# Shared row loads, ten token tiles and one weight sequence in a convolution, MoE and gated-FFN kernel

## The chip, the cores and the metric

The kernel runs on one core of one Trainium2 chip. The metric is the device time of one execution in microseconds. Engines are named as in the profile: PE (TensorE matmul), DVE (VectorE), ACT (ScalarE), POOL (GpSimd), SP (SyncE, which issues all DMAs here).

## The reference

Three layers run one after the other on x of shape (2, 4160, 192). `weight_gen` has shape (2, 4160, 8, 7); d_ff is 1024. The weights of the two feed-forward layers are float64 in memory.

```python
# 1: a causal convolution whose 7 taps differ by token and head
w = softmax(weight_gen, axis=-1)
out = np.einsum('bshk,bskhg->bshg', w, windows_of_7(x))
# 2: token mix, squared ReLU, gate
xk = mu_k * x + (1.0 - mu_k) * x_prev;  xr = mu_r * x + (1.0 - mu_r) * x_prev
k = np.maximum(xk @ w_k, 0.0)
x = sigmoid(xr @ w_r) * (k * k @ w_v)
# 3: a 3-tap convolution along the tokens as the gate of a hidden layer
h = np.maximum(x @ w_in, 0.0)
out = (h * sigmoid(conv3(h, conv_w))) @ w_out
```

## The kernel before

The 4160 tokens of each of the two batches are cut into nine tiles, one of 256 and eight of 488 (lines 15 to 25). Everything is planned by the function of line 169 in units of an abstract time: `at(t, fn)` files an operation under a priority `t`, a tile takes 16 units (line 733), a batch 8, a slice of 128 of the 1024 hidden columns 1. `Program.schedule` (line 101) then orders all operations with a cost for each (line 74): an engine that becomes free takes the operation with the lowest `t` of those that are ready, whether or not a lower one is still to come. What it puts out is a fixed order for each engine's queue.

The work of a tile:

- *Softmax* of the tap weights (line 370): group 0 is tile 0, group 1 is tile 1, group 2 all of tiles 2 to 8 in single instructions. Groups 0 and 1 have scratch of their own, group 2's lies in `stage` (line 232), the space of the weights on their way in.
- *Attention* (lines 402 to 430): `win_load` gives each partition, for two tokens 128 rows apart, all 7 rows of each window (2 x 1344 elements); `att_mul` multiplies two tokens at once, four adds sum the taps into `tok`. Two window buffers. Tile 0's first batch is on DVE, the rest on POOL (lines 717, 720, 736).
- *Mixing* (line 436): PE transposes the tokens into a bank `pa`, ACT shifts them by one token into `att`, DVE forms the two mixes in `mk`, ACT rounds them to the high part, POOL subtracts for the low part; what is left over of the 192 columns goes by DMA into `xB`.
- *First layer* `moe1` (line 526): per slice 5 matmuls into one of two banks `pa`, three ACT steps (ReLU, square, round), one DVE subtraction, 5 matmuls into `am`, `ar`. `gate_r` and `mix_out` put the result into `x2`.
- *Second layer* `moe2` (line 621): per slice 5 matmuls into one of two banks `pc`, ReLU on ACT, the three taps (one on ACT, two on DVE), sigmoid on ACT, product on DVE, rounding on ACT, subtraction on DVE, 5 matmuls into `bm`, `br`. It follows the first layer ten units later (`LAG`).
- *Carry* (line 573) copies the last two columns of `x2` to its front, on POOL.

So one slice through both layers costs 20 matmuls, 7 ACT and 5 DVE instructions. All products are split into a high and a low part.

Each weight is fetched in chunks of 512 or 384 columns into one of two raw buffers of `stage` (line 206), `narrow` (line 271) turns float64 into float32 by one ACT and five DVE instructions in the banks `bm`, `br` and `pc`, and `split` (line 285) writes the high part with ACT and the low part with DVE. Sixteen chunks: `w_k` 3, `w_v` 4, `w_r` 1, `w_in` 3, `conv_w` 1, `w_out` 4, at the priorities of lines 718 to 730. SP issues the loads of windows and weights, the DMAs of `xB` and the stores in one queue.

Of the kernel before, what the change touches and what calls it, by code (L numbers as in the profile page):

```python
# [15 lines left out]
FIRST = 256  # L16
NTILE = 9
REST = (SEQ - FIRST) // (NTILE - 1)
SIZES = [FIRST] + [REST] * (NTILE - 1)
# [4 lines left out]
SLOTS = [2] + [4] * (NTILE - 1)  # L24
# [11 lines left out]
class Program:  # L36
# [7 lines left out]
    def engine(self, name):  # L44
        program = self

        class Engine:
            def __getattr__(self, method):
                return lambda *a, **k: program.ops.append((name, method, a, k, program.now))

        return Engine()
# [22 lines left out]
    def cost(self, eng, method, out, ins, pointer):  # L74
# [21 lines left out]
        if eng == "POOL":  # L96
            busy = 0.06 + (n / 490 if method == "tensor_tensor" else n / 270)
            return busy, busy + 0.16
        return 0.6, 0.6

    def schedule(self):
        n = len(self.ops)
        succ, left, ready, dur, late, moved = [[] for _ in range(n)], [0] * n, [0.0] * n, [0.0] * n, [0.0] * n, [0.0] * n
        log = {}
        for i, (eng, method, a, k, _) in enumerate(self.ops):
# [4 lines left out]
            if method == "dma_start":  # L110
                moved[i] = self.count(out) * out.ap[0][1] * 4 / 200e3 if self.space(out) != "DRAM" else self.count(ins[0]) * ins[0].ap[0][1] * 4 / 200e3
# [18 lines left out]
        free = dict.fromkeys(self.real, 0.0)  # L130
        wires = dict.fromkeys(self.real, 0.0)
# [20 lines left out]
        for i in sorted(range(n), key=lambda i: (start[i], i)):  # L152
            eng, method, a, k, _ = self.ops[i]
            getattr(self.real[eng], method)(*a, **k)  # L154
# [14 lines left out]
def conv_moe_kernel(ctx: ExitStack, tc: tile.TileContext, xp, wg_first, wg_rest, mus, w_k, w_v, w_r, w_in, conv_w, w_out, out):  # L169
# [35 lines left out]
    stage = new("stage", [128, 4608], U32)  # L205
    raw_r = Ring([stage[:, 1024 * j:1024 * j + 1024].rearrange("p (a b) -> p a b", b=2) for j in (0, 1)])
    wy_r = Ring([stage[:, 2048 + 512 * j:2560 + 512 * j] for j in (0, 1)])
    wx_r = Ring([stage[:, 3072:3584]])
    wb_r = Ring([stage[:, 3584:4608].rearrange("p (a b) -> p a b", a=2).bitcast(F32R)])
    win_r = ring("win", 2, [128, 2, WIN])  # L210
# [15 lines left out]
    soft_at = [0, slots[0], slots[0] + slots[1], sum(slots)]  # L226
# [3 lines left out]
    for j in range(3):  # L230
        n = soft_at[j + 1] - soft_at[j]
        flat = new(f"smz{j}", [128, 2 * n * NH]) if j < 2 else f(stage)[:, :2 * n * NH]
# [11 lines left out]
    def at(t, fn):  # L244
        plan.append((t, len(plan), fn))
# [9 lines left out]
    def fetch(w, parts, n):  # L255
# [8 lines left out]
        else:  # L264
            st["x"] = f(wx_r())
# [26 lines left out]
    def prep_in(t, src, A, B, twin):  # L292
        st = {}

        def rem():
            st[0] = fetch(src, lambda w, k: [(64 * h, 64 * h + 64, 0, cols(w, k, 128, 192, 512 * h, 512)) for h in range(2)], 512)

        def rem2():
            x = narrow(st[0], 512)
# [12 lines left out]
        def main(c):  # L312
            st[1 + c] = fetch(src, lambda w, k: [(0, 128, 0, cols(w, k, 0, 128, 512 * c, 512))], 512)

        def main2(c):
            sl = slice(512 * c, 512 * c + 512)
            split(A[:, 0, sl], A[:, 1, sl], narrow(st[1 + c], 512))

        at(t[0], rem)
        at(t[1], rem2)  # L320
        for c in range(2):
            at((t[1] - 1.95, t[1] + 0.02)[c], lambda c=c: main(c))
            at(t[2 + c], lambda c=c: main2(c))

    def prep_out(t, src, W):
        st = {}
        for c in range(4):
            def load(c=c):
                st[c] = fetch(src, lambda w, k: [(0, 128, 0, w[256 * c:256 * c + 256, :].rearrange("(k p) d -> p k d", p=128))], 2 * DM)

            def go(c=c):
                x = narrow(st[c], 2 * DM).rearrange("p (k d) -> p k d", k=2)
                k = slice(2 * c, 2 * c + 2)
                split(W[:, k, 0, :], W[:, k, 1, :], x[:, :, 0:128])
                split(W[:, k, 2, 0:64], W[:, k, 2, 64:128], x[:, :, 128:192])

            at(t[c] - 1, load)
            at(t[c], go)

    def prep_r(t):  # L340
        st = {}

        def load():
            st[0] = fetch(w_r, lambda w, k: [(0, 128, 0, cols(w, k, 0, 128, 0, DM))]
                          + [(64 * h, 64 * h + 64, k * DM, cols(w, k, 128, 192, 0, DM)) for h in range(2)], 2 * DM)

        def go():
            x = narrow(st[0], 2 * DM)
# [4 lines left out]
        at(t - 1, load)  # L353
        at(t, go)

    def load_conv(t):
        st = {}

        def load():
            st[0] = fetch(conv_w, lambda w, k: [(0, 128, 0, w)], 3 * NF)  # L360

        def go():
            DVE.tensor_copy(cw.rearrange("p k n -> p (k n)"), narrow(st[0], 3 * NF))

        at(t, load)
        at(t + 1, go)

    def softmax(j, wg, eng, load, times):  # L370
        w, m, z = sm[j]
        P, n = PART[min(j, 1)], w.shape[1]
        w, m, z = w[:P], m[:P], z[:P]

        def s0():
# [442 lines left out]
```

## Time and profile before

| | |
|---|---|
| time, median of 3 runs | 827.6 us (825.28 to 828.04) |
| the profiled execution | 829.09 us, of which the span of the trace is 827.3 us |
| busy in the span | PE 703.2, PE weight loads 579.4, DVE 633.2, ACT 637.3, POOL 461.7 us |
| mean granted TensorE clock | 0.950 |
| DMA | 73.09 MB, of which the window loads are 34 of 1344 KB |

Read the time by stretch first: shares over the whole span mix a ramp in which weights are prepared, a long steady part and a tail. A matmul's busy time contains its pipeline, so the pace is read from the number of matmuls in a stretch, not from the time of one. Nearly every instruction has line 154, where the planner puts it out, so groups are told apart by tile names. In a timeline the bracket says how long the engine stood idle before the instruction and what ended that.

### The profile page before, as it was taken

The page shows a single profiled execution, that of the slowest core. Times are in us where ns is not written, and L with a number is a line of the kernel's source. Part 1 is how long each engine was busy: PE and PEld are TensorE (multiplying, and loading weights), DVE is VectorE, ACT ScalarE, POOL GpSimd, SP SyncE. Part 2 cuts the span into 40 slices and gives each one's busy share as a digit, 9 for nine tenths or more (in the row PEclk, how much of TensorE's full clock was granted, in tenths as well). Part 3 has the DMA queues.
Part 4 walks back from the last instruction along what each step waited for, and adds up shares of the span by engine and source line. Part 5 has one row for each costly group of instructions (what it writes and reads, how often), then busy time and mean ns, then how long its engine had stood idle before and what let it go on. Part 6 is the DMA issues. An engine that isn't in the chain of part 4 may idle for free.

```text
span 827.3 us, 9620 instructions
## 1 busy us (share of the span) xinstructions
PE 703.2 (85%) x3162; PEld 579.4 (70%) x3162; DVE 633.2 (77%) x1018; ACT 637.3 (77%) x1264; POOL 461.7 (56%) x250
## 2 busy tenths in 40 slices
PE   0145654689899999999999999999999999999775
PEld 0044543578668888888888888788888888888553
DVE  7765858876886878788778878787888787877754
ACT  1244645597797989898989889898989898989653
POOL 3499314586899697898987888969311010100000
PEclk9996787798999999999999999999999999999967
DMA  7654740012423423326126123430020002000000
GB/s 278 215 162 136 231 107 0 1 52 102 151 55 129 152 62 139 134 66 202 59 94 201 75 77 134 134 133 19 19 50 19 1 20 48 19 1 19 0 19 19
DMA packets 24370, 73.09 MB, mean 88 GB/s; under 512 B 3072, under 2 KB 13696, under 8 KB 24192
## 3 DMA queue, kind: packets, MB, share of 16 engines
q1 hardware_dynamic: 24320, 72.47, 26.8%
q8 instruction: 25, 0.41, 0.2%
q14 instruction: 25, 0.20, 0.1%
HBM read 55.45 MB, written 6.39 MB: 75 GB/s over the span
## 4 chain that ended last, share of the span: by engine, by line
PE 61%; DVE 18%; ACT 14%; POOL 4%; issue 2%; DMA 1%; SPq 1%; ACTq 0%; DVEq 0%; POOLq 0%
PE pa L154 18%; PE pc L154 15%; PE am L154 9%; PE bm L154 7%; PE ar L154 6%; DVE pc L154 5%; PE br L154 5%; POOL win L154 3%; ACT h L154 2%; DVE stage L154 2%; ACT g L154 2%; ACT pa L154 2%; ACT x L154 2%; ACT pc L154 1%; DVE g L154 1%
## 5 line engine op out<-in xcount | busy, mean ns | idle before, releaser
L154 DVE SCALAR_TENSOR_TENSOR pc<-h,cw,pc 128x488 f32<-128x488 f32 (+2 forms) x288 | 201.5, 700 | 41.5 <-ACT pc L154 38.4
L154 POOL TENSOR_TENSOR win<-win,sw 128x2688 f32<-128x2688 f32 x33 | 197.7, 5991 | 28.7 <-DMA win<-in_x_dram 28.6
L154 ACT ACTIVATE pa<-pa 128x488 f32<-128x488 f32 (+1 forms) x288 | 155.2, 542 | 53.1 <-PE pa L154 49.8
L154 PE MATMUL bm<-g,wo 128*128 128x488 f32 (+2 forms) x432 | 145.6, 386 | 26.7 <-ACT g L154 26.7
L154 PE MATMUL am<-s,wv 128*128 128x488 f32 (+1 forms) x432 | 144.8, 392 | 25.0 <-ACT s L154 23.0
L154 POOL TENSOR_TENSOR win<-win 128x384 f32<-128x384 f32 (+1 forms) x99 | 153.9, 1575 | 1.5
L154 DVE TENSOR_TENSOR pc<-h,pc 128x488 f32<-128x488 f32 (+2 forms) x144 | 92.3, 641 | 57.6 <-ACT pc L154 56.7
L154 PE MATMUL pa<-xA,wkA 128*128 128x488 f32 (+1 forms) x432 | 120.9, 388 | 15.7 <-DVE mk L154 9.2
L154 PE MATMUL pc<-x,wiA 128*128 128x490 f32 (+2 forms) x432 | 121.2, 385 | 2.4 <-DVE g L154 2.4
L154 PEld LDWEIGHTS bm<-g,wo 128*128 128x128 f32 x432 | 82.5, 195 | 48.2 <-ACT g L154 35.1
L154 DVE TENSOR_TENSOR s<-pa,s 128x488 fp32r<-128x488 f32 (+1 forms) x144 | 91.1, 634 | 30.0 <-ACT s L154 27.6
L154 PEld LDWEIGHTS am<-s,wv 128*128 128x128 f32 x432 | 83.1, 199 | 43.4 <-ACT s L154 28.9
L154 PE MATMUL ar<-s,wv 128*128 128x488 f32 (+1 forms) x288 | 109.4, 389 | 4.1 <-ACT x L154 2.9
L154 PE MATMUL br<-g,wo 128*128 128x488 f32 (+2 forms) x288 | 109.5, 381 | 1.4 <-DVE ob L154 1.4
L154 DVE TENSOR_TENSOR g<-pc,g 128x488 fp32r<-128x488 f32 (+2 forms) x144 | 91.5, 636 | 21.7 <-ACT g L154 20.8
L154 ACT ACTIVATE h<-pc 128x490 f32<-128x490 f32 (+2 forms) x144 | 81.3, 565 | 31.5 <-PE pc L154 26.3
L154 PEld LDWEIGHTS pa<-xA,wkA 128*128 128x128 f32 x432 | 80.9, 198 | 31.3 <-ACT xA L154 8.0
L154 ACT ACTIVATE pc<-h,cw 128x488 f32<-128x488 f32 (+2 forms) x144 | 94.4, 656 | 1.5
L154 PEld LDWEIGHTS pc<-x,wiA 128*128 128x128 f32 x432 | 80.6, 195 | 17.3 <-DVE g L154 4.7
L154 ACT ACTIVATE pc<-pc 128x488 f32<-128x488 f32 (+2 forms) x144 | 78.2, 543 | 15.2 <-DVE pc L154 15.1
L154 POOL TENSOR_TENSOR xA<-mk,xA 128x488 fp32r<-128x488 f32 (+1 forms) x36 | 42.3, 1185 | 84.5 <-ACT xA L154 84.5
L154 PE MATMUL pa<-xB,wkB 128*128 128x488 f32 (+1 forms) x288 | 86.7, 381 | 1.9 <-DMA xB<-mk 1.8
(89 smaller groups left out, 1005.9 us busy)
## 6 DMA issues: line engine op xcount, KB each, us to landing
win<-in_x_dram SPq DMA_DIRECT2D x34, 1344.0 KB, 6.0
xB<-rm SPq DMA_DIRECT2D x32, 122.0 KB, 2.3
xB<-mk SPq DMA_DIRECT2D x32, 122.0 KB, 2.3
out_dram<-om SPq DMA_DIRECT2D x14, 244.0 KB, 2.1
out_dram<-ob SPq DMA_DIRECT2D x14, 122.0 KB, 2.3
sw<-in_rest_dram SPq DMA_DIRECT2D x1, 1568.0 KB, 13.5
stage<-in_moe_w_v_dram SPq DMA_DIRECT2D x4, 384.0 KB, 3.5
stage<-in_moe_w_out_dram SPq DMA_DIRECT2D x4, 384.0 KB, 3.1
```

The costliest lines, as they stand in the source:

```text
L154: getattr(self.real[eng], method)(*a, **k)
```

## The change

- Ten tiles: 256, 248, seven of 472, 352. The two short tiles have two token slots a partition, the last has three.
- Neighbouring tokens lie on one partition: for L tokens it loads L + 6 rows once (`rows`), and each token multiplies its 7 rows into one buffer `prod`; three adds sum the taps. Transposes write with a step of L columns. All attention is on POOL.
- Softmax in four groups: tile 0, tile 1, tile 2, and tiles 3 to 9. The last is loaded late and worked in pieces of one tile each; its scratch lies in `stage`.
- All weight chunks form one sequence with three raw buffers; a chunk's load comes right behind the use of the chunk three before it. `wb` lies in `x2[1]`.
- Mixing of tiles 0 and 1 scales the shifted tokens on ACT and needs one DVE step fewer; for tile 0 the mixes lie in the banks `am` and `ar` and DVE forms the low parts. The carry is on ACT.
- The planner knows a start time for an operation (`hold`), ACT's table loads, and that POOL and a DVE instruction with two SBUF inputs exclude each other; its costs for POOL and DMA are changed.

The diff, cut:

```diff
-SIZES = [FIRST] + [REST] * (NTILE - 1)
+SIZES = [256, 248] + [472] * 7 + [352]
-SLOTS = [2] + [4] * (NTILE - 1)
+SLOTS = [2, 2] + [4] * 7 + [3]
...
-            busy = 0.06 + (n / 490 if method == "tensor_tensor" else n / 270)
-            return busy, busy + 0.16
+            busy = 0.1 + (n / 455 if method == "tensor_tensor" else n / 270)
+            return busy, busy + 0.12
...
+            shares[i] = eng == "POOL" or eng == "DVE" and (
+                src == ["SBUF", "SBUF"] or method in ("tensor_scalar", "tensor_copy") and self.space(out) == "SBUF" and src == ["SBUF"])
...
+            if shares[i]:
+                t = max(t, port)
+                port = t + dur[i]
+            turn = 0.0
+            if eng == "ACT" and self.ops[i][1] == "activation" and self.ops[i][2][2] in (ACTF.Exp, ACTF.Sigmoid):
+                turn = 0.0 if self.ops[i][2][2] == table else 1.3
+                table = self.ops[i][2][2]
...
-    raw_r = Ring([stage[:, 1024 * j:1024 * j + 1024].rearrange("p (a b) -> p a b", b=2) for j in (0, 1)])
+    raw_r = Ring([stage[:, 1024 * j:1024 * j + 1024].rearrange("p (a b) -> p a b", b=2) for j in range(3)])
-    win_r = ring("win", 2, [128, 2, WIN])
+    rows_r = ring("rows", 2, [128, max(SLOTS) + PAD, DM])
+    prod = new("prod", [128, WIN])
...
-    soft_at = [0, slots[0], slots[0] + slots[1], sum(slots)]
+    soft_at = [sum(slots[:j]) for j in (0, 1, 2, 3, NTILE)]
...
+    def prepare(first, seq):
+        for j, (t, (load, n, go)) in enumerate(seq):
...
+            at(first[j] if j < 3 else seq[j - 3][0] + 0.001, ld)
+            at(t, use)
...
+    def attention(i, b, t_load, t, dt_, eng, hold=(0.0, 0.0)):
+        L = SLOTS[i]
+        def load():
+            rows_t[i, b] = rows_r()[:, :L + PAD]
+            row = b * (SEQ + PAD) + STARTS[i] - EXTRA[i]
+            SP.dma_start(out=rows_t[i, b], in_=bass.AP(tensor=xp.tensor, offset=xp.offset + row * DM, ap=[[L * DM, PART[i]], [1, (L + PAD) * DM]]))
+        def token(l):
...
+            eng.tensor_tensor(p.rearrange("p (k g h) -> p k g h", k=KS, h=NH),
+                              rows_t[i, b][:, l:l + KS].rearrange("p k (g h) -> p k g h", h=NH), w, op=ALU.mult)
+            eng.tensor_tensor(y[:, 0:3], y[:, 0:3], y[:, 3:6], op=ALU.add)
+            eng.tensor_tensor(y[:, 0:2], y[:, 0:2], y[:, 2:7:4], op=ALU.add)
+            eng.tensor_tensor(tok_t[i][:, l, b * DM:b * DM + DM], y[:, 0], y[:, 1], op=ALU.add)
...
-                PE.transpose(p[:, l * P:(l + 1) * P], x[:P, l, k:k + 128], ident[:P, :P])
+                PE.transpose(p[:, l:l + SLOTS[i] * (P - 1) + 1:SLOTS[i]], x[:, l, k:k + 128], ident)
...
+            st[k] = (am_r, ar_r)[k]() if i == 0 else mk_r()
+            if i < 2:
+                a = shifted(lambda y, x: ACT.activation(y, x, ACTF.Copy, scale=onemu[:, own]))
+                DVE.scalar_tensor_tensor(out=st[k][:, :N], in0=st["p"], scalar=mu[:, own], in1=a, op0=ALU.mult, op1=ALU.add)
...
-            POOL.tensor_tensor(y, st[k][:, :N], f(x[:, 0, :N]), op=ALU.subtract)
+            (POOL if i else DVE).tensor_tensor(y, st[k][:, :N], f(x[:, 0, :N]), op=ALU.subtract)
...
-                POOL.tensor_copy(x2[b][:, :, 0:2], f(x2[b][:, :, n:n + 2]))
+                ACT.copy(x2[b][:, :, 0:2], f(x2[b][:, :, n:n + 2]))
...
+    attention(0, 0, -99.9, -90, 0.1, POOL)
+    attention(0, 1, -99.6, -83.7, 0.1, POOL)
+    prepare((-99.75, -99.7, -99.4), [(-82, chunk_rem(w_k, wkB, True)), (-81, chunk_in(w_k, wkA, 0)),
+                                     (-0.5, chunk_out(w_v, wv, 0)), (0.4, chunk_out(w_v, wv, 1)), (1.0, chunk_in(w_k, wkA, 1)),
+                                     (1.4, chunk_out(w_v, wv, 2)), (2.4, chunk_out(w_v, wv, 3)), (3.4, chunk_r()),
+                                     (4.4, chunk_rem(w_in, wiB, False)), (5.0, chunk_in(w_in, wiA, 0)), (6.0, chunk_out(w_out, wo, 0)),
+                                     (6.4, chunk_conv()), (7.0, chunk_in(w_in, wiA, 1)), (8.0, chunk_out(w_out, wo, 1)),
+                                     (9.0, chunk_out(w_out, wo, 2)), (10.0, chunk_out(w_out, wo, 3))])
+    softmax_load(3, wg_rest[:, (slots[1] + slots[2]) * KH:], 10.2, 40.0)
+    for j in range(NTILE - 3):
+        a, b = (sum(slots[3:3 + k]) for k in (j, j + 1))
+        softmax(3, a, b, POOL, (16.5 + 0.3 * j, 16.6 + 0.3 * j, 19.5 + 0.1 * j, 20.5 + 0.5 * j, 20.6 + 0.5 * j, 24.9 + 16 * j), None)
...
-                attention(i, b, T - 19.3 + 4.5 * b, T - 15 + 4.5 * b, 2.25, POOL)
-            for u, t in ((0, T - 5), (2, T - 3.7), (1, T + 3)):
+                attention(i, b, T - 22 + 4.5 * b, T - 15 + 4.5 * b, 1.125, POOL, (25.0 + 8 * b if i == 1 else 0.0, 0.0))
+            for u, t in ((0, T - 5), (2, T - 3.7), (1, T + 3)) if i > 1 else ((0, 7), (2, 8.3), (1, 15)):
                 mixing(i, u, t, 2.5)
```

## Rows read from the trace of the kernel before

**Rows 1.** Busy time by stretch: from:to, length, busy (instructions), clock, DMA, GB/s.

```profile
0.00:160.00 160.00, 67.70 (x302) 55.64 (x303) 114.83 (x191) 68.75 (x162) 82.93 (x50) 0.84 0.47 146
160.00:240.00 80.00, 72.39 (x359) 59.51 (x358) 61.00 (x114) 64.85 (x141) 66.54 (x31) 0.96 0.26 87
240.00:760.00 520.00, 515.50 (x2341) 430.18 (x2340) 416.96 (x654) 467.71 (x897) 312.20 (x171) 1.00 0.24 81
760.00:827.00 67.00, 47.56 (x166) 34.06 (x164) 40.42 (x62) 36.03 (x67) 0.00 (x0) 0.82 0.04 12
```

**Rows 2.** Timeline of PE, neighbouring matmuls of 256 columns: start us, us, operation, tiles, shapes.

```profile
164.51 0.28 PE L154 MATMUL bm<-g,wo 128*128 128x256 f32 x1
164.63 0.28 PE L154 MATMUL br<-g,wo 128*128 128x256 f32 x1
```

**Rows 3.** Waits of SP's queue: us in total, times, longest us.

```profile
SPq L154 <- POOL tok L154: 195.3, 26, 21.4
```

**Rows 4.** Timeline of SP: start us, us, engine, line, operation.

```profile
69.48 14.29 SPq L154 DMA_DIRECT2D stage<-in_moe_w_in_dram  x4
```

**Rows 5.** Timeline of DVE: start us, us, operation, tiles, shapes, count, [idle before].

```profile
5.83 0.39 DVE L154 TENSOR_TENSOR sw<-sw,smz 128x224 f32<-128x224 f32 x1
8.15 2.96 DVE L154 TENSOR_TENSOR win<-win,sw 128x2688 f32<-128x2688 f32 x1 [1.93 <-DMA win<-in_x_dram]
...
14.08 5.67 DVE L154 TENSOR_TENSOR win<-win 128x384 f32<-128x384 f32 x1
...
77.23 0.57 DVE L154 TENSOR_SCALAR br<-br 128x384 uint32<-128x384 uint32 x1 [2.75 <-ACT br L154]
...
126.45 5.76 DVE L154 TENSOR_REDUCE stage<-sw 128x448 f32<-128x3136 f32 x1
...
140.03 0.28 DVE L154 TENSOR_TENSOR wo<-br,wo 128x128 fp32r<-128x128 f32 x1
```

**Rows 6.** Timeline of POOL.

```profile
13.49 5.84 POOL L154 TENSOR_TENSOR win<-win,sw 128x2688 f32<-128x2688 f32 x1 [12.07 <-DMA win<-in_x_dram]
...
132.30 6.84 POOL L154 TENSOR_TENSOR sw<-sw,stage 128x3136 f32<-128x3136 f32 x1 [26.76 <-DVE stage L154]
...
153.70 6.92 POOL L154 TENSOR_TENSOR sw<-sw,stage 128x3136 f32<-128x3136 f32 x1 [12.17 <-DVE stage L154]
160.71 12.00 POOL L154 TENSOR_TENSOR win<-win,sw 128x2688 f32<-128x2688 f32 x2
```

**Rows 7.** Groups by shape, attention on POOL.

```profile
L154 POOL TENSOR_TENSOR win<-win,sw 128x2688 f32<-128x2688 f32 x33 | 197.7, 5991 | 28.7 <-DMA win<-in_x_dram 28.6
...
L154 POOL TENSOR_TENSOR win<-win 128x384 f32<-128x384 f32 x66 | 66.5, 1022 | 0.5
```

**Rows 8.** Groups by shape, weight chunks on DVE: busy us, mean ns | idle before.

```profile
L154 DVE SCALAR_TENSOR_TENSOR stage<-stage,pc 128x384 f32<-128x384 uint32 x9 | 5.0, 550 | 0.2
L154 DVE SCALAR_TENSOR_TENSOR stage<-stage,pc 128x512 f32<-128x512 uint32 x6 | 4.1, 682 | 0.1
```

**Rows 9.** Groups by shape, ACT and DVE on the two tile sizes.

```profile
L154 ACT ACTIVATE pa<-pa 128x488 f32<-128x488 f32 x256 | 143.6, 564 | 35.6 <-PE pa L154 32.6
...
L154 DVE SCALAR_TENSOR_TENSOR pc<-h,cw,pc 128x256 f32<-128x256 f32 x32 | 15.6, 486 | 5.0 <-ACT pc L154 4.5
...
L154 ACT ACTIVATE pa<-pa 128x256 f32<-128x256 f32 x32 | 11.6, 371 | 17.5 <-PE pa L154 17.2
...
L154 DVE TENSOR_TENSOR s<-pa,s 128x256 fp32r<-128x256 f32 x16 | 6.6, 420 | 10.9 <-ACT s L154 10.8
```

**Rows 10.** Timeline of PE in the tail, two slices apart.

```profile
804.40 0.71 PE L154 MATMUL bm<-g,wo 128*128 128x490 f32 x2 [2.01 <-ACT g L154]
...
812.17 0.71 PE L154 MATMUL bm<-g,wo 128*128 128x490 f32 x2 [2.01 <-ACT g L154]
```

**Rows 11.** Timeline of ACT around the big exponential.

```profile
139.77 1.28 ACT L154 ACT_TABLE_LOAD   x1
141.06 2.82 ACT L154 ACTIVATE sw<-sw 128x3136 f32<-128x3136 f32 x1
143.90 1.28 ACT L154 ACT_TABLE_LOAD   x1
145.20 0.37 ACT L154 ACTIVATE pc<-pc 128x256 f32<-128x256 f32 x1
```

More of the change, by code (lines that the diff above doesn't have):

```diff
@@ L130, in schedule @@
         free = dict.fromkeys(self.real, 0.0)
+        port, table = 0.0, None
         wires = dict.fromkeys(self.real, 0.0)
@@ L290, in cols, with chunk_rem, go @@
         return w[p0:p1, k * c0:k * (c0 + n)]
[L292 to L299, printed above, removed]
+    def chunk_rem(src, B, twin):
+        def go(x):
             y = wb_r()
@@ L351, in go, with chunk_conv, ld, use @@
                 ACT.copy(W[:, :, DM:256], f(W[:, :, 128:DM]))
[L353 to L375, printed above, removed]
-            SP.dma_start(out=w.rearrange("p s k h -> p (s k h)"), in_=wg)
+        return lambda: fetch(w_r, lambda w, k: [(0, 128, 0, cols(w, k, 0, 128, 0, DM))]
+                             + [(64 * h, 64 * h + 64, k * DM, cols(w, k, 128, 192, 0, DM)) for h in range(2)], 2 * DM), 2 * DM, go
+    def chunk_conv():
+        return lambda: fetch(conv_w, lambda w, k: [(0, 128, 0, w)], 3 * NF), 3 * NF, lambda x: ACT.copy(cw.rearrange("p k n -> p (k n)"), x)
+    def prepare(first, seq):
+        for j, (t, (load, n, go)) in enumerate(seq):
+            st = {}
+            def ld(st=st, load=load):
+                st[0] = load()
+            def use(st=st, n=n, go=go):
+                go(narrow(st[0], n))
+            at(first[j] if j < 3 else seq[j - 3][0] + 0.001, ld)
+            at(t, use)
+    def softmax_load(j, wg, t, hold=0.0):
+        w = sm[j][0]
+        at(t, lambda: SP.dma_start(out=w.rearrange("p s k h -> p (s k h)"), in_=wg), hold)
+    def softmax(j, a, b, eng, times, bank):
+        w, m, z = (x[:, a:b] for x in sm[j])
+        n = b - a
+        if bank is not None:
+            z = bank[:, :n * NH].rearrange("p (s h) -> p s h", s=n)
         def fold(dst, op):
@@ L418, in att_add @@
[L418 to L430 removed]
+    rows_t, tok_t = {}, {}
@@ new lines, in attention @@
+    def attention(i, b, t_load, t, dt_, eng, hold=(0.0, 0.0)):
[5 more added lines that the diff above has]
+        def token(l):
+            if i not in tok_t:
+                tok_t[i] = tok_r()
+            p = prod
+            y = p.rearrange("p (k d) -> p k d", k=KS)
+            w = sw[:, sum(slots[:i]) + b * L + l].unsqueeze(2).to_broadcast([128, KS, DM // NH, NH])
+            eng.tensor_tensor(p.rearrange("p (k g h) -> p k g h", k=KS, h=NH),
[3 more added lines that the diff above has]
+            eng.tensor_tensor(tok_t[i][:, l, b * DM:b * DM + DM], y[:, 0], y[:, 1], op=ALU.add)
+        at(t_load, load, hold[0])
+        for l in range(L):
+            at(t + l * dt_, lambda l=l: token(l), hold[1])
@@ L748, in conv_moe_kernel @@
             store(i, b, t + LAG + 10.02)
-    for t, _, fn in sorted(plan, key=lambda e: e[:2]):
-        prog.now = t
+    for t, _, fn, hold in sorted(plan, key=lambda e: e[:2]):
+        prog.now, prog.hold = t, hold
         fn()
```

158 lines of the change are left out of this document (58 added, 100 removed).

## The prediction

> **What bounds the kernel now.** Read the busy time by stretch first [rows 1]. From 240 to 760 us TensorE is busy 515.5 of 520 us at clock 1.00, 2341 matrix instructions, 0.222 us for each: there PE is the bound, and only fewer or shorter matmuls would help. The other three rows are different. Up to 160 us PE is busy 67.7 us with 302 instructions, at a mean clock of 0.84; from 160 to 240 it runs 359 instructions. After 240 us 2501 of the 3162 instructions are left; at 0.222 us they are 555 us and would end at 795.5. The span ends at 827.3, so the tail loses 32 us. At PE's own pace all 3162 would take 702 us, 35 us less because tile 0's 340 are narrower (0.118 us at 256 columns [rows 2]): 667. So some 128 us are lost in the first 240 us. That is where the change can win.
>
> What ends last there? Second view, the waits of SP's queue: it stood 195 us, in 26 waits, for the attention to free a window buffer [rows 3]. SP issues in order, so weight loads behind such an issue wait too: four issues of w_in that need little over 2 us of issue time are spread over 14.3 us [rows 4]. Third, VectorE's order of time [rows 5]. It has tile 0's softmax done at 6.2 us, does half of tile 0's attention, and then the weights, chunk by chunk; the last piece of the last chunk (wo) ends at 140.3. On the way it stands still (2.75 us before the row at 77.23), while ACT waits for a chunk that has not landed. At 14.08 an add of 384 elements takes 5.67 us: it reads two SBUF operands beside GpSimd's multiply of 13.49 to 19.33 and ends only with it [rows 5, 6]. Fourth, POOL [rows 6]: 26.8 us and 12.2 us idle before the two big softmax steps, and tile 2's attention starts at 160.7, because the softmax of tiles 2 to 8 uses the weights' staging space and comes when the weights are done.
>
> **The change, part by part.**
>
> *Loads of shared rows.* A load for tile 0 falls from 1344 KB to 768 KB, for a whole tile and batch from two of 1344 KB to one of 960 KB; the issues fall from 34 to 20. The same elements are multiplied and added. For one token POOL ran half of a 2688 multiply (5.99 us) and half of one 1152 and three 384 adds [rows 7]; one multiply of 1344 with adds of 576, 384 and 192 has two more starts per pair. A line through the two rows (2688 in 5.99, 384 in 1.02) has a fixed part of 0.19 us, so a pair costs 11.6 + 3 x 0.19 = 12.2, a token 6.1 us. A 472 tile costs POOL 8 x 6.1 + 7.4 for its six low-part subtractions + 1.2 of softmax = 57 us against some 76 us of PE: hidden. Its cover is gone only in the ramp, priced below.
>
> *Tile 0's attention on POOL alone.* Four tokens, 24.4 us from about 7 us on, end at 31.5; before, DVE and POOL together ended at 25.5. DVE is freed of 14 us of window work, some of it the stretched add. GpSimd took 5.84 us for the multiply that DVE did in 2.96 [rows 5, 6]. The Trainium skill (GPSIMD Engine Reference, 4.1 Engine selection) says that elementwise work on two inputs belongs on VectorE, GPSIMD being about twice slower; this trace agrees (1.97). By that rule the start would come 6 us later, and the time would be 792 if the start hung on attention. I add nothing, since the weights come much later than 31 us.
>
> *Weights in one sequence, three buffers.* Six chunks of 512 columns cost six DVE operations of 0.682, 4.1 us each; nine of 384 cost five of 0.55 and splits of about 0.71, 3.5 us each [rows 8]; the small one 1 us: 57 us in all, as before. What goes is the waiting: window loads stand no longer in SP's queue in front of weight loads unless their rows are late, and three raw buffers let a load of 2 us or more run beside two chunks. Conv's copy goes to ACT, 0.2 us, nothing.
>
> *Stage A, to the last chunk.* DVE has 57 of weights, 7 of softmax groups 0 to 2, 8.4 of mixing for tiles 0 and 1 (12 operations of 0.486, 6 of 0.42), and 10 of tile 0's first layer (24 of 0.42) [rows 9]: 82 us, from 6 us on. In the first 160 us of before DVE was busy 72% [rows 1]; between that (120 us) and 100% (88) I take 94%, because its known waits, the loads and the GpSimd collision, are what the change removes: the last chunk ends at 93 us instead of 140. The second layer cannot start before: its PSUM banks are those that the weights are converted in.
>
> *Stage B, tile 0's second layer beside tile 1's first.* Per slice of 256 columns DVE has 2 x 0.486 + 3 x 0.42 = 2.2 us, ACT 7 x 0.371 = 2.6, PE 20 x 0.118 = 2.4 [rows 2, 9]. Sixteen slices: 36, 42 and 38 us. Added on DVE: mixing out and stores 8, tile 2's mixing 6, group 3's softmax 18 (two folds of 5.76 [rows 5] and 3.3 of reciprocal before, now in pieces); 68 us. On ACT: 16 us. Between 42 (PE with its gates and transposes) and 68 I take 60: most of group 3 serves tiles that come much later, and some of it can slide. *Stage C, tile 1's second layer beside tile 2's first:* PE 16 x (10 x 0.118 + 10 x 0.215) plus gates, 57 us; DVE 51, ACT 56. Tile 2's rows must be there by 153: POOL has 31.5 + 3 (group 1) + 26.7 (tile 1, group 2) + 4.4 + 48.8 + 8 (group 3's subtractions) = 122 if nothing stalls it. So tile 2's first layer ends at 93 + 60 + 57 = 210.
>
> *The steady part.* Left are 160 + 6 x 352 instructions at 472 columns and 349 at 352. From 0.118 at 256 and 0.222 at 488 [rows 1, 2] the slope is 0.00045 us a column: 0.215 and 0.161. 2272 x 0.215 + 349 x 0.161 = 545 us. ACT's fixed part is 0.157 us (0.371 at 256, 0.564 at 488 [rows 9]); the tenth tile adds 112 ACT instructions, 17.6 us, off the bound in the steady part and inside B and C. Moving the carry to ACT adds a copy of 8 columns, 20 times, whose source and reader are long done; at nothing, or 0.2 us each without that cover. Transposes now write with a step; the trace has none like it; 105 at 0.13, between no cost and twice, so 0 to 14 us, near 0, for each lies among matmuls that write as many columns.
>
> *The tail.* Two slices of the last tile take 7.77 us [rows 10]. With 138 columns fewer through some nine dependent steps of about 0.001 us a column, 6.5. Twelve slices: 47 becomes 39 us, and PE's own work in them 26.6 becomes 19.3. The loss stays near 31 us.
>
> Sum: 210 + 545 + 31 = 786 us of span. The profiled execution took 829.1 with a span of 827.3, and the median of three is 827.6: 1.8 on, 1.5 off. Forecast **786 us**.
>
> **The rivals.** *Ramp quicker.* Group 3 slides behind as a whole, B is PE's 42 and A is the 88 of a full DVE: 786 - 18 - 5 = 763. For: 160 to 240 us shows 359 matmuls in 80 us with DVE at 76% and ACT at 81% [rows 1]. Against: nothing is idle enough to promise it.
>
> *Activation tables.* The one big exponential becomes seven. Before, it stood between two table loads of 1.28 us [rows 11]. If each of the seven is placed alone among sigmoids, that is 14 loads instead of 2, 15.4 us more on ACT in stage B, where it holds 58: about 801. For: they become ready one after the other as POOL reaches them. Against: once several are ready they go in a row. The Trainium skill (ScalarE: Activation LUTs, What ACT_TABLE_LOAD costs, and Table sets: the hidden batching unit) asks to batch by table set and counts a drain of about 1380 ns beside each load, 2.66 us a switch; by that it would be 32 us and 818. The rows show the next ACT instruction within 0.02 us of a load's end, so the smaller price stands.
>
> *POOL behind group 3.* Its subtractions share space with the last weight chunk and stand in POOL's queue ahead of tile 2's tokens. If POOL stops there until 94, tile 2 comes at 94 + 57 = 151 and is mixed at 157: 4 us late; with tokens at 6.5 us, 12: 790 to 798.
>
> *Slower: the chunks are no sooner ready.* If what set the weights' pace was the hand-over between ACT and DVE within a chunk and not the loads, the last chunk ends near 140 again, and then the time is that end plus 693: 833. Slower than before from an end of 137 on, since the change has one more narrow tile to pass through the slow stage; at 145 it is 838. For: four chunks between 77.2 and 98.2 took 21 us where DVE's share was 16. Against: the same figure, 5.3 a chunk, gives 85 us for sixteen, not 130. That the change does not do what it says is this case too.
>
> **How the numbers follow.** Forecast with its POOL variant 0.55 (770 to 800), quicker ramp 0.2, tables 0.13, weights late in part (105 to 130 us, 798 to 823) 0.06, slower 0.06. Low: quicker ramp with A at 84 and B at 42, 759, less the start, 755. High: tables and 12 us of POOL, 813, with a little for the stepped writes: 815. A measurement tells about 0.3%, 2.5 us, from no change. Faster 0.92, within 0.02, slower 0.06.
>
> **What would show it.** The last wo subtraction on DVE near 93 us (85 to 100) and no stretched add of window or token on DVE; SP's waits for the attention far below 195 us; seven exponentials in at most three runs between tables; tile 2's last token on POOL between 115 and 150; about 0.215 us an instruction in the middle; PE busy by 210 us with over 860 instructions done, where before had about 550. If DVE ends the weights past 120 us, or PE shows gaps of microseconds between 210 and 740, the forecast is wrong.

## The result and the profile after

The changed kernel takes 790.77 us (median of four runs, 789.52 to 793.36), the kernel before 827.45 (825.28 to 828.04): a ratio of 0.9565 with the 95% interval [0.9536, 0.9595]. The forecast was 786. The profiled execution took 793.36 us with a span of 791.6, granted clock 0.973.

Busy time by stretch in the changed kernel; the columns are those of [rows 1]. The last line holds the count on which most of this study rests, PE's instructions done by 210 us.

```profile
0.00:93.00 93.00, 39.39 (x195) 33.68 (x195) 74.67 (x165) 48.40 (x129) 74.54 (x67) 0.91 0.63 183
93.00:160.00 67.00, 49.48 (x325) 45.68 (x324) 54.10 (x121) 60.47 (x149) 59.98 (x46) 0.85 0.10 36
160.00:210.00 50.00, 49.70 (x313) 45.26 (x314) 38.93 (x87) 45.39 (x120) 47.88 (x34) 1.00 0.20 64
240.00:700.00 460.00, 457.40 (x2162) 395.78 (x2161) 374.73 (x609) 418.70 (x842) 293.43 (x203) 1.00 0.14 41
0.00:210.00 210.00, 138.57 (x831) 124.62 (x832) 167.70 (x370) 154.26 (x396) 182.41 (x145) 0.91 0.36 108
```

PE has run 831 matrix instructions by 210 us (548 before). From 240 to 700 it is full at clock 1.00, 460 / 2162 = 0.213 us for each. The gain is in the ramp, as forecast: the middle only works off what is left.

PE and DVE, timeline: the first matmul of the second layer, and the last piece of the last weight chunk, which answers to the last line of [rows 5].

```profile
82.05 0.85 PE L167 MATMUL pc<-x,wiA 128*128 128x258 f32 x3
...
89.13 0.28 DVE L167 TENSOR_TENSOR wo<-br,wo 128x128 fp32r<-128x128 f32 x1
```

The last chunk ends at 89.4 us instead of 140.3. POOL, timeline: first tokens of tiles 0, 1 and 2, and the last one of tile 2; [rows 6] had tile 2 begin at 160.71.

```profile
9.14 3.01 POOL L167 TENSOR_TENSOR prod<-rows,sw 128x1344 f32<-128x1344 f32 x1 [7.76 <-DMA rows<-in_x_dram]
...
39.42 3.02 POOL L167 TENSOR_TENSOR prod<-rows,sw 128x1344 f32<-128x1344 f32 x1
...
69.49 3.04 POOL L167 TENSOR_TENSOR prod<-rows,sw 128x1344 f32<-128x1344 f32 x1
...
137.21 3.07 POOL L167 TENSOR_TENSOR prod<-rows,sw 128x1344 f32<-128x1344 f32 x1
```

And ACT: all table loads by form, then one of the six places in the timeline where exponentials of group 3 stand between two of them.

```profile
L167 ACT ACT_TABLE_LOAD x14 | 18.0, 1283 | 5.2 <-DMA sw<-in_first_dram 5.0
...
111.90 1.28 ACT L167 ACT_TABLE_LOAD   x1
113.19 0.58 ACT L167 ACTIVATE sw<-sw 128x448 f32<-128x448 f32 x1
113.79 1.28 ACT L167 ACT_TABLE_LOAD   x1
115.08 0.37 ACT L167 ACTIVATE pc<-pc 128x256 f32<-128x256 f32 x1
```

Seven exponentials between 92.8 and 131.8 us, five with a pair of loads each and the last two sharing one: twelve loads (the expectation of the next run counts 13). This is the tables rival, with ten loads more than before instead of twelve, and its price was not the 15 us it named.

### The profile page after: what moved, and what is told of

Its sections match the earlier page's. It is cut to its first block, busy times and chain, and to the rows that moved or that the text cites. A ratio compares the mean times of both kernels' runs of the same rounds, so it can differ in the third digit from the quotient of the medians.

```text
span 791.6 us, 10781 instructions
## 1 busy us (share of the span) xinstructions
PE 697.2 (88%) x3505; PEld 607.3 (77%) x3505; DVE 631.4 (80%) x1137; ACT 666.5 (84%) x1441; POOL 506.2 (64%) x368
## 4 chain that ended last, share of the span: by engine, by line
PE 68%; ACT 15%; DVE 13%; issue 2%; DMA 2%; SPq 0%; ACTq 0%; DVEq 0%
PE pa L167 21%; PE pc L167 16%; PE am L167 10%; PE bm L167 9%; PE ar L167 7%; PE br L167 5%; DVE pc L167 4%; ACT pa L167 2%; ACT pc L167 2%; DVE stage L167 2%; ACT h L167 2%; ACT g L167 2%; ACT L167 1%; DMA stage<-in_moe_w_k_dram 1%; DVE bm L167 1%
## 5 line engine op out<-in xcount | busy, mean ns | idle before, releaser
L167 DVE SCALAR_TENSOR_TENSOR pc<-h,cw,pc 128x472 f32<-128x472 f32 (+3 forms) x320 | 208.1, 650 | 39.5 <-ACT pc L167 36.7
L167 POOL TENSOR_TENSOR prod<-rows,sw 128x1344 f32<-128x1344 f32 x70 | 216.1, 3087 | 12.8 <-DMA rows<-in_x_dram 7.8
L167 ACT ACTIVATE pa<-pa 128x472 f32<-128x472 f32 (+3 forms) x320 | 160.8, 505 | 39.1 <-PE pa L167 35.2
L167 POOL TENSOR_TENSOR prod<-prod 128x576 f32<-128x576 f32 (+1 forms) x140 | 171.0, 1221 | 8.6
L167 PE MATMUL bm<-g,wo 128*128 128x472 f32 (+3 forms) x480 | 148.7, 360 | 21.3 <-ACT g L167 21.1
L167 PE MATMUL am<-s,wv 128*128 128x472 f32 (+3 forms) x480 | 147.0, 367 | 7.1 <-ACT s L167 5.8
L167 PE MATMUL pa<-xA,wkA 128*128 128x472 f32 (+3 forms) x480 | 125.9, 368 | 7.5 <-DVE s L167 3.4
L167 PE MATMUL pc<-x,wiA 128*128 128x474 f32 (+3 forms) x480 | 121.6, 361 | 3.5 <-DVE g L167 3.5
L167 PE MATMUL ar<-s,wv 128*128 128x472 f32 (+3 forms) x320 | 112.6, 364 | 4.9 <-DVE x L167 3.3
L167 PE MATMUL br<-g,wo 128*128 128x472 f32 (+3 forms) x320 | 112.4, 355 | 1.4 <-DVE ob L167 1.4
L167 ACT ACTIVATE pc<-h,cw 128x472 f32<-128x472 f32 (+3 forms) x160 | 99.7, 623 | 1.8
```

## The experiments

The theory to be tested is the prediction's: the weights, held up in SP's queue, set when the second layer starts, POOL's idleness sets when tile 2 comes, and the table loads are what the forecast missed. Its rivals are named in each expectation. One thing holds for all runs: the planner orders every kernel anew, so an edit changes the order of other work too. A measured price contains that, and prices need not add up. The table loads move with the order as well: 14 in the change, 10 with the old tile sizes and with tile 0 on DVE, 8 with the windows and with the old planner, 6 with two raw buffers, 4 with three groups. So each of these prices holds fewer loads too. Times are medians; ratios are against the kernel before, run beside.

### One exponential for group 3

```diff
         def s3():
-            ACT.activation(w, w, ACTF.Exp)
+            if j < 3:
+                ACT.activation(w, w, ACTF.Exp)
+            elif b == sm[3][0].shape[1]:
+                ACT.activation(sm[3][0], sm[3][0], ACTF.Exp)
...
-        softmax(3, a, b, POOL, (16.5 + 0.3 * j, 16.6 + 0.3 * j, 19.5 + 0.1 * j, ...
+        softmax(3, a, b, POOL, (16.5 + 0.3 * j, 16.6 + 0.3 * j, 19.5, ...
```

> The seven exponentials of softmax group 3 are one instruction again, behind all seven subtractions; everything else is the changed kernel (790.8 us). Theory (table loads stand on the path between 93 and 137 us, where the trace shows 13 of them at 1.28 us on ACT and PE waiting for ACT's g beside them): ten loads fall away, 12.8 us of ACT, and the time is 776 to 782 us. Rival (the forecast's own sum: VectorE sets that stretch and the loads lie beside its work): 787 to 791 us.

782.01 us (781.29 to 784.68), ratio 0.946 [0.9435, 0.9485]: 8.8 us less than the change, the fastest kernel of the study. Its ACT timeline, and its stretches to 93 and to 210 us:

```profile
103.72 1.28 ACT L167 ACT_TABLE_LOAD   x1
105.01 2.73 ACT L167 ACTIVATE sw<-sw 128x3024 f32<-128x3024 f32 x1
107.75 1.28 ACT L167 ACT_TABLE_LOAD   x1
...
0.00:93.00 93.00, 40.61 (x219) 34.47 (x219) 78.22 (x172) 51.33 (x137) 77.42 (x70) 0.93 0.60 183
0.00:210.00 210.00, 143.42 (x879) 127.02 (x880) 176.86 (x386) 151.69 (x400) 183.35 (x145) 0.95 0.35 109
```

Four table loads in the whole kernel instead of fourteen, and 879 PE instructions by 210 us: 48 more, at 0.213 us 10 us. So the rival, no gain, is out, and the time meets the theory's upper edge. But the price is not pure. The last chunk, ahead of all these loads, already ended 3.6 us earlier (85.8) by the new order, and PE is 24 instructions ahead at 93 us, where the first of the loads stood in the change. About 5 of the 8.8 us are left for the loads themselves (an estimate: 8.8 less 3.6); most of that shows from 110 to 135 us, with 136 PE instructions instead of 84. Ten loads of 1.283 are 12.8 us of ACT time, so that not all of it was on the path. The Trainium skill (ScalarE: Activation LUTs, What ACT_TABLE_LOAD costs) counts 2.66 us a switch with its drain, which for ten would be an estimated 26.6 us. No row here shows the drain: the next ACT instruction starts 0.01 us behind a load's end, and the whole gain is a third of that figure.

### Two raw buffers, and the old tile sizes

```diff
-    raw_r = Ring([... for j in range(3)])
+    raw_r = Ring([... for j in range(2)])
...
-            at(first[j] if j < 3 else seq[j - 3][0] + 0.001, ld)
+            at(first[j] if j < 2 else seq[j - 2][0] + 0.001, ld)
```

> The changed kernel with two raw buffers instead of three in the weight sequence. Theory of the forecast (SP's queue standing behind window loads made the weights late, the third buffer only helps): last chunk between 89 and 97 us, time 790 to 797 us. Rival (the buffers are the gain: each load of about 4 us is waited for): last chunk between 100 and 112 us, time 800 to 812 us.

791.13 us (789.24 to 792.2), ratio 0.9562 [0.9538, 0.9586]: no difference to the change. The time is the theory's and the end of the last chunk the rival's, so neither explains both. Its DVE timeline and its table loads by form:

```profile
100.65 0.27 DVE L167 TENSOR_TENSOR wo<-br,wo 128x128 fp32r<-128x128 f32 x1
...
L167 ACT ACT_TABLE_LOAD x6 | 7.7, 1283 | 3.4 <-DMA sw<-in_first_dram 3.3
```

The last chunk ends 11.5 us later and ACT loads 8 tables less (10.3 us). Two opposite effects may cancel here; that the third buffer alone is worth nothing is not shown. What is shown: the end of the last chunk does not set the time by itself.

```diff
-SIZES = [256, 248] + [472] * 7 + [352]
+SIZES = [256] + [488] * 8
-SLOTS = [2, 2] + [4] * 7 + [3]
+SLOTS = [2] + [4] * 8
```

> The changed kernel with the nine tiles of before, 256 and eight of 488 (one transposing step of tile 1 is filed later, behind its four tokens). Theory (the sizes are worth little: the tenth tile costs about what the narrow second tile gives the ramp; tile 1's rows need 48 us of POOL and come near 93 us, when the second layer starts): 783 to 796 us. Rival (the short second tile is what lets the first layer run ahead while the weights come): 803 to 815 us.

790.63 us (788.87 to 792.23), ratio 0.9563 [0.9533, 0.9593]. One priority of tile 1's mixing is 9.4 instead of 8.3 here. The narrower tiles, 343 more instructions and a shorter tail, come to nothing in sum, as the theory said.

### Softmax groups

In the change without a group for tile 2:

```diff
-    soft_at = [sum(slots[:j]) for j in (0, 1, 2, 3, NTILE)]
+    soft_at = [sum(slots[:j]) for j in (0, 1, 2, NTILE)]
...
+    softmax_load(2, wg_rest[:, slots[1] * KH:], 10.2, 40.0)
+    softmax(2, 0, sum(slots[2:]), POOL, (11.5, 11.55, 11.6, 11.65, 11.7, 11.75), None)
```

> The changed kernel with the softmax in three groups as before it: tiles 2 to 9 in single instructions, loaded and worked when the weights are done. Theory (POOL idle until the big group has passed the weights' space is what tile 2 waited for; a tile group of its own removes it): tile 2's first token moves from about 95 us to 130 or later, its first layer to 190 or later, and the time rises by 10 to 22 us over the change, to 800 to 812, although the seven table switches become one. Rival (tile 2 is in time anyway, the weights set the start, and the one exponential saves its switches): 776 to 788.

807.07 us (805.38 to 808.54), ratio 0.9744 [0.9718, 0.977]: 16.3 us more, though the tables are loaded four times only. POOL's timeline, and the stretch to 210 us:

```profile
88.02 7.64 POOL L167 TENSOR_TENSOR sw<-sw,stage 128x3472 f32<-128x3472 f32 x1 [19.95 <-DVE stage L167]
...
113.02 7.63 POOL L167 TENSOR_TENSOR sw<-sw,stage 128x3472 f32<-128x3472 f32 x1 [16.01 <-DVE stage L167]
120.73 3.08 POOL L167 TENSOR_TENSOR prod<-rows,sw 128x1344 f32<-128x1344 f32 x1
...
0.00:210.00 210.00, 128.63 (x750) 113.85 (x751) 152.18 (x318) 129.86 (x346) 151.23 (x111) 0.87 0.34 103
```

POOL is idle 20 and 16 us ahead of the two big steps, as in [rows 6], and tile 2's first token comes at 120.7, not 69.5 (the expectation had it past 130, and near 95 in the change). 81 PE instructions fewer by 210 us are 17 us. The last chunk ends at 89.2 as in the change, so this loss has nothing to do with the weights.

The same part alone in the kernel before:

```diff
-    softmax(2, wg_rest[:PART[1], slots[1] * KH:], POOL, 11.42, (11.5, 11.55, 11.6, 11.65, 11.7, 11.75))
+    softmax(2, wg_rest[:, slots[1] * KH:(slots[1] + slots[2]) * KH], DVE, -97.9, (0.9, 0.91, 0.92, 0.93, 0.94, 0.95))
+    softmax(3, wg_rest[:, (slots[1] + slots[2]) * KH:], POOL, 11.42, (11.5, 11.55, 11.6, 11.65, 11.7, 11.75))
```

> The kernel before with one part of the change alone: tile 2 gets a softmax group of its own, worked long before the weights are done (its steps on DVE in the order of priorities, scratch shared with tile 1's group); tiles 3 to 8 stay one group in single instructions. Theory (POOL's idle 39 us ahead of tile 2 cost the kernel before): tile 2's attention starts before 120 us instead of 160.7 and the time falls by 10 to 22 us, to 806 to 818. Rival (the weights, ready at 140 us, set the start, and tile 2 would wait for them anyway): 820 to 830, no change beyond 1 per cent.

823.48 us (822.98 to 823.85), ratio 0.9943 [0.9925, 0.996]: about 5 us, the theory's time missed, the rival's met. DVE's timeline:

```profile
146.94 4.98 DVE L154 TENSOR_REDUCE stage<-sw 128x384 f32<-128x2688 f32 x1 [2.74 <-ACT sw L154]
151.83 0.42 DVE L154 TENSOR_TENSOR wo<-br,wo 128x256 fp32r<-128x256 f32 x1
152.16 3.48 DVE L154 TENSOR_SCALAR stage<-stage 128x384 f32<-128x384 f32 x1
...
155.96 0.28 DVE L154 TENSOR_TENSOR wo<-br,wo 128x128 fp32r<-128x128 f32 x1
```

Tile 2's attention does start early (99.6 us), but the last chunk slips from 140.3 to 156.2. SP issues its load only 4.5 us later than before (at 124.8 instead of 120.3). The rest is lost on DVE, where a fold of the later group and a step stretched to 3.48 us (0.38 in the kernel before, for 448 elements) stand ahead of the last pieces. So the loss is not mainly SP's queue, to which the expectation of the joint run below puts it. That what the rows gain is lost there is likely but not shown.

### Loads

Window loads issued by GpSimd in the kernel before:

```diff
-            at(t_load + q * dt_, lambda l=l: win_load(i, b, l, SP))
+            at(t_load + q * dt_, lambda l=l: win_load(i, b, l, POOL))
```

> The kernel before with the window loads issued by GpSimd, whose own additions free the window buffers, instead of SyncE; nothing else is changed. The weight loads no longer stand behind a window load that waits for its buffer. Theory (SP's queue, 195 us of waits for the attention, set the pace of the weights): the last weight chunk ends before 120 us instead of 140.3 and the time falls by 10 to 25 us, to 803 to 818. Rival (the hand-over between ACT and DVE within each chunk and DVE's own work set that pace): the last chunk at 132 or later and the time 818 to 830, possibly above 830, since GpSimd pays for 34 issues.

810.74 us (808.85 to 811.59), ratio 0.9786 [0.9764, 0.9808]: 17.8 us less, the last chunk at 112.4 (`112.16 0.28` on DVE). So the window loads in SP's queue did hold the weights up. With the tile 2 group added to this kernel:

> The kernel before with both single parts: tile 2's own softmax group, and the window loads issued by GpSimd. Alone the first gave 5 us (its trace has the last weight chunk at 156 us instead of 140, behind tile 2's window loads in SP's queue) and the second 18 us (last chunk at 112). Theory (two limits one behind the other: the weights in SP's queue hide what tile 2's early rows are worth): more than the sum, the last chunk again before 118 us, tile 2's first layer before 185 us, and 790 to 800. Rival (they add up, or less): 803 to 811.

813.02 us (811.94 to 816.27), ratio 0.983 [0.9799, 0.986]: no better than the queue alone and 2 us above even the rival's range, so the theory of two limits in series falls. POOL's timeline shows why:

```profile
111.13 5.90 POOL L154 TENSOR_TENSOR sw<-sw,stage 128x2688 f32<-128x2688 f32 x1 [8.40 <-DVE stage L154]
...
133.45 1.22 POOL L154 TENSOR_TENSOR xA<-mk,xA 128x488 fp32r<-128x488 f32 x1 [14.03 <-ACT xA L154]
135.27 5.88 POOL L154 TENSOR_TENSOR sw<-sw,stage 128x2688 f32<-128x2688 f32 x1 [0.60 <-DVE stage L154]
...
143.47 5.97 POOL L154 TENSOR_TENSOR win<-win,sw 128x2688 f32<-128x2688 f32 x1
```

The group of tile 2 is ready, but the order written out puts both big steps of tiles 3 to 8 and tile 1's subtractions in front of tile 2's first multiply, with 14 us of idleness between. With the queue alone that multiply came at 141.7 us, so the early group has not moved it forward. An early group helps here only if nothing late is queued ahead of the work that it frees. In the change the later group is in pieces of 1.14 us.

The reverse, the change with the old loads (windows, two tokens to a multiply, four slots in the last tile). A first version loaded the windows of tiles 2 to 9 ahead of its two buffers, so that some were overwritten before they were multiplied, and those tiles are computed from wrong rows; in 5 to 100 us its loads wait only 3.7 us for the attention:

> The changed kernel with the old loads: each token's seven rows from memory in windows of two tokens 128 rows apart, two tokens to a multiply, transposes without a step, and four token slots in the last tile; group order, weight sequence, tiles and planner stay those of the change, and all attention stays on GpSimd. Theory (shared rows save DMA bytes and issues that hide behind other work; the order of softmax and weights is what counts): 788 to 800. Rival (the shared rows are what frees SP's queue for the weights): the last weight chunk past 105 us, and 805 to 825.

812.6 us (808.39 to 814.04), ratio 0.9803 [0.9771, 0.9835], with the last chunk at 109.4: the rival's time and sign, but of a kernel that does other work. With loads in the order of the buffers:

```diff
-SLOTS = [2, 2] + [4] * 7 + [3]
+SLOTS = [2, 2] + [4] * 8
...
-            SP.dma_start(out=rows_t[i, b], in_=bass.AP(tensor=xp.tensor, offset=xp.offset + row * DM, ap=[[L * DM, PART[i]], [1, (L + PAD) * DM]]))
+        queue.dma_start(out=w[:P], in_=bass.AP(tensor=xp.tensor, offset=xp.offset + row * DM, ap=[[DM, P], [P * DM, 2], [1, WIN]]))
...
-                PE.transpose(p[:, l:l + SLOTS[i] * (P - 1) + 1:SLOTS[i]], x[:, l, k:k + 128], ident)
+                PE.transpose(p[:, l * P:(l + 1) * P], x[:P, l, k:k + 128], ident[:P, :P])
...
-                attention(i, b, T - 22 + 4.5 * b, ...
+                attention(i, b, T - (22 if i == 1 else 19.3) + 4.5 * b, ...
```

> The changed kernel with the old window loads, as the run before, but a window is loaded only when its buffer's last tokens are multiplied, at the priorities of the kernel before. The run without that order stood at 812.6 with the last chunk at 109 us. Theory formed after that run (windows bring SP's queue its old waits and the DMA queues 28 MB more; the weights come later): the last chunk at 105 to 125 us, SP's waits for the attention in the first 100 us above 20 us, and 805 to 822. Rival (what counts is the order, not the loads): the last chunk before 97 us and 788 to 800.

807.15 us (806.01 to 808.04), ratio 0.9749 [0.9722, 0.9776]: 16.4 us more than the change, as expected, but the two signs are missed. The last chunk ends at 102.2, between theory and rival, and SP waits 12.4 us for the attention in 5 to 100 us, not over 20:

```profile
SPq L167 <- POOL tok L167: 12.4, 4, 8.3
...
0.00:210.00 210.00, 131.47 (x764) 118.04 (x765) 166.62 (x349) 135.22 (x363) 166.34 (x102) 0.85 0.44 144
```

The loads are worth 16 us in the change; how much of it is SP's queue, the 76.0 MB against 45.1, attention in coarser pieces, or PE's clock (granted 0.66 from 93 to 160 us, against 0.85 in the change), is not told apart.

### Tile 0's attention on DVE

```diff
-    attention(0, 0, -99.9, -90, 0.1, POOL)
+    attention(0, 0, -99.9, -90, 0.1, DVE)
```

> The changed kernel with the first batch of tile 0's attention on VectorE, in a product buffer of its own (space of tile 1's tokens, still unused then). The prediction added nothing for that attention on GpSimd. Theory (the weights on VectorE set the start, so each us of attention there delays them): tile 0's tokens come 8 to 14 us earlier, the last chunk 2 to 8 us later, and the time is 0 to 5 us longer than the change, 790 to 796. Rival (GpSimd, about twice as slow, holds the start up): 779 to 787.

797.64 us (794.73 to 799.09), ratio 0.9633 [0.9604, 0.9662]: 6.9 us more, 1.6 over the theory's range. The first-layer matmuls start at 34.2 instead of 42.5, and the last chunk ends at 96.2 instead of 89.4. DVE's and POOL's timeline:

```profile
7.28 1.56 DVE L167 TENSOR_TENSOR tok<-rows,sw 128x1344 f32<-128x1344 f32 x1 [0.52 <-DMA rows<-in_x_dram]
...
12.46 4.36 DVE L167 TENSOR_TENSOR tok<-rows,sw 128x1344 f32<-128x1344 f32 x1
...
12.39 3.01 POOL L167 TENSOR_TENSOR prod<-rows,sw 128x1344 f32<-128x1344 f32 x1 [11.01 <-DMA rows<-in_x_dram]
15.48 2.60 POOL L167 TENSOR_TENSOR prod<-prod 128x576 f32<-128x576 f32 x1
```

Alone the multiply takes 1.56 us on DVE; beside POOL's it takes 4.36 and stretches POOL's next add to 2.60 (mean 1.43). Giving all of it to GpSimd was right.

### The planner

The new planner's knowledge (table loads, the shared space of POOL and DVE, costs) in the kernel before, and the old one's in the change:

```diff
-            if shares[i]:
-                t = max(t, port)
-                port = t + dur[i]
...
-                turn = 0.0 if self.ops[i][2][2] == table else 1.3
+                turn = 0.0
```

> The kernel before with the change's planner alone: table loads, the shared space of GpSimd and VectorE, and the costs of GpSimd and DMA; priorities, tiles, loads, groups and weights stay. Theory (the order the planner finds is set by the priorities; the costs move little): 820 to 832. Rival (the planner keeps VectorE from stretched adds and orders the ramp better): 805 to 818.

813.46 us (812.81 to 814.57), ratio 0.983 [0.9807, 0.9853]: 14.7 us less than before, where nothing of the work itself is changed. My theory falls; the rival's time is met, but not by fewer stretched adds: the one of [rows 5] is there again (`14.03 6.00` on DVE).

> The changed kernel with the planner's knowledge of the kernel before: old costs of GpSimd and DMA, no table loads, no shared space of GpSimd and VectorE; start times, priorities, loads, groups, weights and tiles stay. The new planner alone took 15 us off the kernel before. Theory (it gives the order in which engines meet, in this kernel too): stretched adds on VectorE in the first 100 us, the last chunk past 92 us, and 797 to 808. Rival (the other parts have removed the collisions that the planner went around): 786 to 795.

811.99 us (810.81 to 813.25), ratio 0.9813 [0.9781, 0.9845]: 21.2 us more than the change and 4 over the theory's range, the last chunk at 104.8. DVE's waits for ACT's rounding `s` in the first 160 us (total, times, longest), in the order before, before with the new planner, after, after with the old one:

```profile
DVE s L154 <- ACT s L154: 12.9, 8, 3.2
```
```profile
DVE s L167 <- ACT s L167: 5.2, 6, 1.9
```
```profile
DVE s L167 <- ACT s L167: 3.4, 5, 1.3
```
```profile
DVE s L164 <- ACT s L164: 11.7, 9, 2.6
```

All of DVE's waits for ACT in that stretch add up to 36.6, 29.1, 22.8 and 30.1 us. With the old costs DVE waits for ACT some 7 us longer in both kernels; that this is what costs 14.7 and 21.2 us is not shown. The theory's stretched adds are missed: with the old planner too, no DVE instruction of the first 100 us takes over 1 us. In the changed kernel with the old planner there is one more loss, far behind the ramp: the timelines of POOL, DVE and PE, and the stretch to 210 us.

```profile
308.14 1.18 POOL L164 TENSOR_TENSOR xA<-mk,xA 128x472 fp32r<-128x472 f32 x1
...
309.35 0.71 DVE L164 SCALAR_TENSOR_TENSOR mk<-att,onemu,pa 128x472 f32<-128x472 f32 x1 [5.54 <-POOL xA L164]
...
312.61 1.55 PE L164 MATMUL pa<-xA,wrA 128*128 128x472 f32 x3 [6.48 <-DVE mk L164]
...
0.00:210.00 210.00, 132.01 (x784) 117.70 (x784) 160.86 (x355) 140.19 (x370) 177.40 (x141) 0.89 0.35 108
```

47 instructions fewer by 210 us are 10 us; another 6.5 are lost at 312, where the mixing of a steady tile waits for a subtraction on POOL. ACT has that subtraction's input ready at 297.4 us, but in POOL's order it stands behind further tokens. POOL is no fuller than in the change, which has no gap here: from 280 to 320 us it is busy 38.6 us, and 38.3 in the change. So this loss is the order again. Which of the planner's three pieces of knowledge does it was not tried.

### One count behind most of the times

For the kernels with the change's tiles, the count by 210 us forecasts the span from the change's 791.6 at 0.213 us an instruction:

| kernel | PE instructions by 210 us | span so forecast | measured |
|---|---|---|---|
| one exponential | 879 | 781.4 | 780.7 |
| two raw buffers | 848 | 788.0 | 789.9 |
| tile 0 on DVE | 817 | 794.6 | 796.2 |
| windows | 764 | 805.9 | 805.7 |
| three groups | 750 | 808.9 | 805.1 |
| old planner | 784 | 801.6 | 809.5, with the gap at 312 us |

The last chunk's end would not do it: 100.9 us with two raw buffers at 789.9, 89.2 with three groups at 805.1.

## Why the prediction was nearly right

*The sum.* 884 instructions were to be done by 210 us, 831 were: 53 x 0.213 = 11.3 us late. The steady part ran at 0.213 instead of 0.215 on 2272 instructions: 5 us back. 786 + 11.3 - 5 = 792.3 against a span of 791.6. With one exponential the ramp does 879, nearly the forecast's figure. The two errors partly cancel, which is luck, and the sign of over 860 instructions was missed. The term that was mis-sized is stage B and C together: 117 us forecast, about 132 measured, from the last chunk at 89.4 to the 884th instruction near 221. With one exponential the same stretch is about 125 us (85.8 to 211). The table loads, which the forecast put into at most three runs of exponentials where six came, are thus about half of the 15 us; by these readings; what the rest is stays open. The loads had a chance of 0.13 at 801; the mechanism came, with ten loads more instead of twelve and 8.8 us at most instead of 15.4.

*Stage A.* 89.4 us for 93: right, within the stated 85 to 100, and no window or token add is stretched (no DVE instruction takes over 1.02 us before 100). Its reasons were half right. DVE was busy 74.7 of the first 93 us, not 82 of 87: less work and more idleness cancelled, so the figure itself is partly luck. The window loads ahead of the weights were a true cause (17.8 us in the kernel before). But the 195 us of SP's waits [rows 3], from which the argument started, were a total over the span, and of POOL's attention alone. In 5 to 100 us SP of the kernel before waited for the attention 27.0 us, more than half of it for tile 0's batch on DVE:

```profile
SPq L154 <- DVE tok L154: 14.6, 1, 14.6
SPq L154 <- POOL tok L154: 12.4, 3, 8.0
```

That is close to the 27.9 us by which the last chunk came earlier when only these loads left the queue (140.3 to 112.4). After, SP waits 0.9 us in that stretch (0.6 for POOL's `tok`, 0.3 for its `prod`, the multiply that frees the rows). Over the span, `prod` still holds it for 171.4 us, and that is not "far below 195". As a total the sign was ill chosen: SP may wait long where it has nothing else to issue.

*The second layer "cannot start before" the last chunk.* It did, at 82.05 against 89.4, and the trace of the kernel before already had it so: the first of these matmuls at 125.75 against 140.3. The chain A, B, C was too strict as a series. With two raw buffers the last chunk came 11.5 us later in the same time, though with eight table loads less.

*The planner* had no term in the sum at all, and undoing it costs 21 us, more than any other part. The forecast assumed that the new order would be near what the engines can do; it gave no price for the case that it is not.

*Softmax groups.* Right: POOL's idleness ahead of tile 2 was worth 16.3 us in the changed kernel. The tokens came later than worked out: tile 0's end at 39.3 instead of 31.5, because softmax steps of groups 1 and 2 stood among them and POOL started at 9.1, not 7; tile 2's last at 143.5, inside 115 to 150, but not 122. Group 3's subtractions in front of tile 2 (the rival of 790 to 798) are part of that: from 90.8 to 99.7 us they stand ahead of its fourth token.

*Attention on POOL.* A token took 6.13 us, worked out as 6.1. Nothing was to be added for it, and the run with DVE says so.

*The rest.* Transposes with a step: 288 ns in the mean against 282, free. Two slices of the last tile take 6.56 us (6.5 forecast). PE by form, and its timeline in the tail:

```profile
L167 PE MATMUL pa<-ident,tok 128*128 128x128 f32 x105 | 18.2, 288 | 42.7 <-POOL tok L167 37.8 <-ACT r L167 2.4 <-DVE mk L167 1.2
...
776.59 0.59 PE L167 MATMUL bm<-g,wo 128*128 128x354 f32 x2 [1.20 <-ACT g L167]
...
783.15 0.60 PE L167 MATMUL bm<-g,wo 128*128 128x354 f32 x2 [1.21 <-ACT g L167]
```

The quicker ramp did not come; nor did the slower case, weights ready near 140. What stays open: undone one at a time, loads, groups and planner cost 16.4, 16.3 and 21.2 us, 54 together where the change gave 37. They are not independent, and no set of shares for them was found.

## What to carry to other kernels

Count the bounding engine's instructions done by the end of the ramp, not the end of one preparation: here that count gave the time within 4 us in five of six kernels. Where an order is fixed ahead by a planner, its costs are a part of the kernel that has a price of its own, and an operation split into pieces to free one engine must be looked at on every engine it passes: one exponential in place of seven, with ten table loads less, gave 8.8 us with all that its new order brought, a fifth of the 45 that this kernel gains. Read waits in the stretch that is lost, not over the span, and for every engine that can hold the buffer.

## What the runs showed of the hardware

PE's clock in the ramp. In the changed kernel, busy time by 10 us:

```profile
65.00:75.00 10.00, 4.70 (x25) 3.53 (x24) 6.73 (x16) 7.08 (x22) 8.34 (x8) 0.73 0.41 142
75.00:85.00 10.00, 7.67 (x32) 7.11 (x33) 9.31 (x22) 5.66 (x16) 9.61 (x9) 0.50 0.32 89
85.00:95.00 10.00, 9.43 (x65) 8.53 (x63) 9.58 (x22) 8.71 (x24) 7.28 (x7) 0.92 0.00 1
```

In the first of these stretches PE is busy 4.7 of 10 us and the granted clock falls (0.73 in the mean); the next is wholly at 0.50, the lower level (1.2 GHz), with 32 instructions in 7.67 us, where 65 fit into 9.43 us behind it. A gap in the ramp so costs more than its length here. From 93 to 160 us the granted clock is 0.85 in the change and 0.95 with one exponential; how much of the 8.8 us came that way is not told apart. Of the kernels with one part of the change undone it is lowest with the old planner (0.76) and the windows (0.66), so their prices hold some of the clock too.

DVE and POOL on two SBUF operands: 4.36 us for 1.56 alone, above. The Trainium skill (SBUF — State Buffer, SBUF: two separate sides) says that whichever starts first holds the shared port for the whole instruction and the other fully blocks; here POOL's multiply of 12.39 to 15.40 started first, and DVE's, 1.56 long, ended at 16.82, 1.42 behind it: the trace agrees.
